# A planned order with other prices for transposes and landings, and earlier dates for loads

## The chip, the cores and the metric

The kernel runs on one core of a Trainium2 chip. The metric is the device time of one launch in microseconds (us), the median of three runs. Beside it there is the span of one profiled execution, from its first to its last instruction; it is about 2 us shorter than the time of that execution.

A core has five engines with instruction streams of their own: PE (TensorE, matmuls), ACT (ScalarE), DVE (VectorE), POOL (GpSimd) and SP (SyncE, which here only issues DMAs). Each executes its stream in order, so an instruction that waits holds up all that stand behind it on its engine.

## The reference, cut to what matters

```python
# q, k, v: 8 batches, 8 heads, 576 rows, 64 wide (float32)
phi = lambda x: np.where(x > 0, x, np.exp(x) - 1.0) + 1.0
q_p, k_p = phi(q), phi(k)
kv = einsum('bhsd,bhse->bhde', k_p, v)
z = sum(k_p, axis=2)
x = einsum('bhsd,bhde->bhse', q_p, kv) / (einsum('bhsd,bhd->bhs', q_p, z) + 1e-6)
# x as 4608 rows of 512; four experts, w1 512 x 1024, w2 1024 x 512
p = domain_probs / (domain_probs.sum(-1) + 1e-9)
out = sum over e of p[:, e] * (relu(x @ w1[e]) @ w2[e])
```

It is a linear attention whose output goes into a mixture of four experts, all of which are computed for every row and added with the weights p.

## The kernel before, in words

**Tiling.** Of the 576 rows of a batch, 512 form four chunks of 128; the other 64 (the "rest") of two batches share a tile. Attention runs per batch b and pair of heads pr: four pairs per batch. A pair loads k, v and q (`load_pair`, tiles kq and vs), takes Exp on ACT (L412), the rest of phi on DVE (L404, L405), casts v on ACT (L408), multiplies k and v on PE (L457, L460), copies the product on ACT (L470, L471), turns q so that its features lie on the partitions (qT, by a DMA transpose of SP at L443 for batches 2 to 7), multiplies again on PE (L481) and divides on DVE (L495 to L504) into x. `load_rest` and `rest_maps` do the same for the 64 rows (tiles kqr, vr; transpose at L334).

**Units.** From about 82 us on the experts run in 64 units (j, s, e): a block of 512 rows j, half of it s, expert e. `prep` scales two chunks by p on ACT (xp, L706) and turns them with one DMA transpose of SP (xT, L708). `xsums` makes sums of xT on DVE (xs, L724). `l1_seven` is the first matrix product with seven block products instead of eight (L746, eight matmuls each), with copies on ACT (L763), Relu on ACT (L760) and Relu with an addition on DVE (L766). `ssums` makes sums of its results on DVE (L808), and `l2_unit` is the second product, seven blocks of four matmuls (L822). After the fourth expert the sums are put together on DVE (L893 to L900) and stored by SP. Batches 0 and 1 and the first block of rows go another way, before 82 us.

**What sets the order.** Nothing is scheduled by hand. Each helper hands small pieces of work to the planner `Plan` by `pl.add(engine, duration, priority, function, r=..., w=..., move=..., after=...)`. `r` and `w` are keys of the buffers that are read and written, and give the dependencies. `Plan.order` then steps through time with a clock of its own: of the pieces that are ready, it takes the one that can start first, and of those within 0.1 us of it the one with the lowest priority. A piece with `move` is a DMA: after its issue (its duration) it goes through one common mover, and its users may start when it has landed. `after` is a time before which a piece isn't placed. The pieces are then emitted by their planned start, each engine in that order; POOL keeps the order of its adds. The planned times don't exist on the chip, only the order.

`T0` = 84 and `TU` = 6.4 are the planner's start of the first unit and its period; `U(n)` = T0 + n TU. `batch(b)` places the loads of batch b at `t - 8` and its attention from `t` on, where t counts backwards from the unit that first needs the batch.

**Buffers.** From batch 2 on, pairs alternate between two staging buffers (kq, vs). xp has two buffers, xT three, qT two.

Of the kernel before, what the change touches and what calls it, by code (L numbers as in the profile page):

```python
# [20 lines left out]
class Plan:  # L21
# [11 lines left out]
        self.wr = {}  # L33
        self.rd = {}

    def add(self, eng, dur, pri, fn, r=(), w=(), move=0.0, after=0.0):
        n = len(self.ops)
        deps = set()
        for key in r:
            if key in self.wr:  # L40
                deps.add(self.wr[key])
            self.rd.setdefault(key, []).append(n)
        for key in w:
            if key in self.wr:
                deps.add(self.wr[key])
            deps.update(x for x in self.rd.get(key, ()) if x != n)
        for key in w:
            self.wr[key] = n
            self.rd[key] = []
        self.ops.append(  # L50
            dict(eng=eng, dur=dur, pri=pri, fn=fn, deps=deps, move=move, after=after, w=w)
        )
        return n

    def order(self):
        ops = self.ops
        left = [len(o["deps"]) for o in ops]
        users = [[] for _ in ops]
        for n, o in enumerate(ops):
            for d in o["deps"]:  # L60
                users[d].append(n)
        free = {o["eng"]: 0.0 for o in ops}
        ready = {e: {} for e in free}
        fixed = {"POOL": [n for n, o in enumerate(ops) if o["eng"] == "POOL"]}
        at = [o["after"] for o in ops]
        mover = 0.0

        def release(n):
            ready[ops[n]["eng"]][n] = at[n]

        for n in range(len(ops)):
            if left[n] == 0:
                release(n)
        start = [0.0] * len(ops)
        for _ in ops:
            best = None
            for e, cand in ready.items():
                if e in fixed:
                    cand = {n: cand[n] for n in fixed[e][:1] if n in cand}
                if not cand:  # L80
                    continue
                t = max(free[e], min(cand.values()))
                if best is None or t < best[0]:
                    best = (t, e, cand)
            t, e, cand = best
            n = min(
                (n for n, x in cand.items() if x <= t + self.NEAR),
                key=lambda n: (ops[n]["pri"], n),
            )
            o = ops[n]  # L90
            del ready[e][n]
            if e in fixed:
                fixed[e].pop(0)
            start[n] = max(t, at[n])
            free[e] = done = start[n] + o["dur"]
            if o["move"]:
                mover = max(done + 1.2, mover) + o["move"]
                done = mover + 0.8
            o["start"], o["done"] = start[n], done
            for u in users[n]:  # L100
                lat = self.HOP if ops[u]["eng"] != e or o["move"] else 0.03
                at[u] = max(at[u], done + lat)
                left[u] -= 1
                if left[u] == 0:
                    release(u)
        return [ops[n] for n in sorted(range(len(ops)), key=lambda n: (start[n], n))]
# [3 lines left out]
def kernel(  # L110
# [10 lines left out]
    nc = tc.nc  # L121
# [10 lines left out]
    DC = Dm // P  # L132
# [5 lines left out]
    T0, TU = 84.0, 6.4  # L138

    pl = Plan()  # L140
# [36 lines left out]
    qTr = [sb(f"qTr{i}", [P, DC, P], FP16) for i in range(2)]  # L177
# [135 lines left out]
    def rest_maps(b, pe_mode, pri, parts=(0, 1)):  # L313

        par = b % 2
        rs = slice(par * R, par * R + R)
        ei = rot("ek", 2)
        er = ek_b[ei].rearrange("p i h c d -> p i (h c) d")

        def maps(i):  # L320
            o = kqpr[rs, i]
            nc.vector.tensor_scalar(o, kqr[rs, i], 0.0, 1.0, AO.max, AO.add)
            nc.vector.tensor_tensor(out=o, in0=er[rs, i], in1=o, op=AO.min)

        for i in parts:
            sk, ek, key = ("str", par, 2 * i), ("ek", ei, i), ("kpr", "qpr")[i]
            pl.add("ACT", 0.55, pri + i * 0.5, lambda i=i: nc.scalar.activation(
                er[rs, i], kqr[rs, i], AF.Exp), r=(sk,), w=(ek,))
            if i == 0:
                pl.add("ACT", 0.55, pri + 0.1, lambda: nc.scalar.copy(  # L330
                    vprs[par][rs, :, 0:D], vr[rs]), r=(("str", par, 1),), w=(("vpr", par),))
            pl.add("DVE", 0.92, pri + 0.5 + i * 0.5, lambda i=i: maps(i), r=(sk, ek), w=(key,))
        if not pe_mode:
            pl.add("SP", 0.45, pri + 1, lambda: nc.sync.dma_start_transpose(  # L334
                out=qTr[par][:, :, rs], in_=kqpr[rs, 1].rearrange("p h d -> p (h d)")),
                r=("qpr",), w=[("qTr", par, i) for i in range(DC)], move=1.2)

    def rest_late(pri):

# [42 lines left out]
    def attention(b, pr, pe_mode, pri, step, two=False):  # L382
# [35 lines left out]
        if pe_mode:  # L418

            tq, tk = (l2b[1].bitcast(FP16), "l2b1") if two else (tbank, "l2b3")  # L420

            def turn():
                for c in range(C):
                    nc.tensor.transpose(
                        out=tq[:, c * P : (c + 1) * P], in_=qp[:, c], identity=identh
                    )
                if two:
                    return
                nc.tensor.transpose(
                    out=tq[:, NT : NT + R],  # L430
                    in_=kqpr[rs, 1, hs].rearrange("p h d -> p (h d)"),
                    identity=identh[rs, rs],
                )

            pl.add("PE", 0.32, pri + 3 * step, turn,
                   r=(("kqp", pi, 1), "ident") + (() if two else ("qpr",)), w=(tk,))
            pl.add("ACT", 0.5, pri + 3.5 * step, lambda: nc.scalar.copy(
                qT.rearrange("p c t -> p (c t)"), tq[:, 0:NT]), r=(tk,), w=(("qT", ti),))
            if not two:
                pl.add("DVE", 0.2, pri + 3.5 * step, lambda: nc.vector.tensor_copy(  # L440
                    qTr[par][:, pr, rs], tq[:, NT : NT + R]), r=(tk,), w=(("qTr", par, pr),))
        else:
            pl.add("SP", 0.45, pri + 3 * step, lambda: nc.sync.dma_start_transpose(  # L443
                out=qT, in_=qp.rearrange("p c h d -> p (c h d)")),
                r=(("kqp", pi, 1),), w=(("qT", ti),), move=1.2)

        kvs_, ndk = slot[0], (("at",), ("at",))
        nds = [slot[0:3], slot[0:2]]
# [243 lines left out]
    def prep(n):  # L692

        j, s, e = units[n]
        xi, ti = n % 2, n % 3
        xp, xT = xp_b[xi], xT_b[ti]
        pri = U(n) - 7.0
        for c in range(2):
            cc = 2 * s + c
            if j < NJ - 1:  # L700
                src, ps = x_b[j % 2][:, cc, :], p_nat[:, j, cc, e : e + 1]
                r = [("x", j % 2, pr, cc) for pr in range(DC)] + ["pnat"]
            else:
                src, ps = xr_sb[:, cc, :], p_rest[:, cc, e : e + 1]
                r = [("xr", b, pr) for pr in range(DC) for b in (2 * cc, 2 * cc + 1)] + ["prest"]
            pl.add("ACT", 0.55, pri, lambda c=c, src=src, ps=ps: nc.scalar.activation(  # L706
                xp[:, c, :], src, AF.Copy, scale=ps), r=r, w=(("xp", xi, c),))
        pl.add("SP", 0.45, pri + 1, lambda: nc.sync.dma_start_transpose(  # L708
            out=xT.rearrange("p c k t -> p (c k) t"), in_=xp.rearrange("p c d -> p (c d)")),
            r=(("xp", xi, 0), ("xp", xi, 1)), w=(("xT", ti),), move=1.7)  # L710

    def xsums(n):
        xi, ti = n % 2, n % 3
        xT, xs = xT_b[ti], xs_b[xi]
        tt = nc.vector.tensor_tensor
        X = lambda i: ("xs", xi, i)
        for i, (o, a, b_, dur, d, r, w) in enumerate((
            (xs[:, 0:2], xT[:, 1].rearrange("p (a k) t -> p a k t", a=2), xT[:, :, 0:2],
             0.42, 0.9, (), (X(0), X(1))),
            (xs[:, 2], xT[:, 1, 2:4], xs[:, 0], 0.25, 1.8, (X(0),), (X(2),)),  # L720
            (xs[:, 3], xT[:, 0, 2:4], xs[:, 2], 0.25, 5.4, (X(2),), (X(3),)),
        )):
            pl.add("DVE", dur, U(n) + d - 1.0,
                   lambda o=o, a=a, b_=b_: tt(out=o, in0=a, in1=b_, op=AO.subtract),  # L724
                   r=(("xT", ti),) + r, w=w)
# [246 lines left out]
    def batch(b):  # L972

        due = U(8 * (b - 1)) - 8
        for pr in range(DC):
            t = due - (DC - pr) * 2 * TU
            if b == 2:
                t = T0 + 4 + 10.5 * pr
            load_pair(b, pr, "SP", t - 8, after=t - 8)
            if pr == 0:  # L980
                load_rest(b, "SP", t - 7, after=t - 7)
                rest_maps(b, False, t - 2)
# [56 lines left out]
```

## Time and profile before

| | |
|---|---|
| time, median of three runs | 508.55 us (507.77 to 510.18) |
| time of the profiled execution | 507.87 us |
| its span | 506.0 us |
| instructions | 14856 |
| TensorE clock granted | 0.997 |
| HBM read, written | 45.16 MB, 9.44 MB |
| SP's DMA queue (q1) | 51.53 MB, 46.0% of 16 engines' span |

The busy time of each engine is the sum over its instructions in the profiled execution. The busy tenths show 40 equal slices of the span, 12.65 us each; a 9 means 90% or more:

```profile
PE   2799999999999999999999999999999999999995
DVE  5787996989898989897979989888987676767664
ACT  5737667877888689758977887789776766676641
POOL 8856400000000000000000000000000000000000
```

Four stages can be seen: the weights come in on POOL's queue up to slice 5; from slice 6 or 7 to about slice 29 attention of batches 2 to 7 runs among the units; then units alone, with DVE and ACT less busy; and a short end.

### The profile page before, as it was taken

To read this page: it belongs to the slowest core of one execution; us is meant where nothing else is said; L and a number is where in the kernel's file an instruction comes from. 1 tells how busy PE (TensorE), PEld (TensorE's weight loads), DVE (VectorE), ACT (ScalarE), POOL (GpSimd) and SP (SyncE) were. 2 spreads that over 40 slices of the span, in tenths; PEclk is the share of its full clock that TensorE was granted. 3 is DMA by queue.
4 is the path that set the end of the run, shared out by engine and by line. 5 is a ranking of instruction groups with operands and counts; after the bars stand their busy time and mean duration, and the time that the engine had idled before them with its cause. 6 is when DMAs were issued, how large, how long until landed. Compare 5 with 4: busy or idle time off the path is not lost.

```text
span 506.0 us, 14856 instructions
## 1 busy us (share of the span) xinstructions
PE 483.4 (96%) x6008; PEld 424.3 (84%) x6008; DVE 409.1 (81%) x1036; ACT 368.3 (73%) x694; POOL 43.0 (8%) x68
## 2 busy tenths in 40 slices
PE   2799999999999999999999999999999999999995
PEld 1444546999989999998989999999999999999995
DVE  5787996989898989897979989888987676767664
ACT  5737667877888689758977887789776766676641
POOL 8856400000000000000000000000000000000000
PEclk9999999999999999999999999999999999999998
DMA  8999929667696767564666475566643232323221
GB/s 242 227 232 225 266 49 233 140 177 162 120 168 126 169 119 166 131 162 110 136 116 146 117 159 159 84 177 144 157 95 85 45 90 48 85 53 85 43 45 43
DMA packets 124006, 67.51 MB, mean 133 GB/s; under 512 B 94480, under 2 KB 117776, under 8 KB 123936
## 3 DMA queue, kind: packets, MB, share of 16 engines
q1 hardware_dynamic: 115056, 51.53, 46.0%
q0 software_dynamic: 8720, 14.76, 13.6%
q8 instruction: 47, 0.77, 0.6%
q10 hardware_dynamic: 160, 0.26, 0.1%
q14 instruction: 23, 0.19, 0.1%
HBM read 45.16 MB, written 9.44 MB: 108 GB/s over the span
## 4 chain that ended last, share of the span: by engine, by line
PE 72%; ACT 9%; DMA 7%; DVE 7%; issue 4%; SPq 2%; DVEq 0%; POOL 0%; POOLq 0%; ACTq 0%
PE l1b L746 29%; PE l2b L822 28%; PE l1b L594 6%; PE l2b L604 5%; DMA kq<-in_q_dram 2%; ACT xp L706 1%; ACT h L760 1%; SPq L232 1%; DMA kqr<-in_q_dram 1%; PE at L481 1%; DVE s L808 1%; DMA xT<-xp 1%; ACT ek L412 1%; DMA kqr<-in_k_dram 1%; PE at L457 1%
## 5 line engine op out<-in xcount | busy, mean ns | idle before, releaser
L746 PEld LDWEIGHTS <-w 128*128 128x128 f16 x2048 | 132.9, 98 | 6.7 <-issue 1.3
L822 PE MATMUL l2b<-w,h 128*128 128x256 f16 x768 | 114.4, 273 | 0.7 <-ACT h L760 0.6
L760 ACT ACTIVATE h<-l1b 128x512 f16<-128x512 f32 x128 | 76.7, 599 | 49.1 <-PE l1b L746 47.8
L822 PE MATMUL l2b<-t,s 128*128 128x256 f16 x768 | 112.3, 273 | 0.0
L746 PEld LDWEIGHTS <-w1x 128*128 128x128 f16 x1536 | 100.1, 98 | 7.5 <-issue 3.9
L822 PEld LDWEIGHTS <-s 128*128 128x128 f16 x1024 | 91.4, 98 | 6.9
L766 DVE CUSTOM_DVE_ANT_0 h<-l1b,p 128x512 f16<-128x512 f32 x64 | 44.2, 690 | 50.4 <-PE l1b L746 49.5
L746 PE MATMUL l1b<-xs,w1x 128*128 128x128 f16 x1024 | 77.7, 219 | 1.8 <-ACT l1b L763 1.7
L746 PE MATMUL l1b<-xs,w 128*128 128x128 f16 x1024 | 78.1, 219 | 1.0 <-ACT u L763 0.6
L706 ACT ACTIVATE xp<-x,p_nat 128x512 f16<-128x512 f16 x112 | 76.2, 721 | 3.3 <-DMA xT<-xp 3.0
L746 PE MATMUL l1b<-xT,w 128*128 128x128 f16 x1024 | 78.1, 219 | 0.1
L822 PEld LDWEIGHTS <-h 128*128 128x128 f16 x768 | 67.3, 98 | 5.9 <-ACT h L760 1.3
L808 DVE TENSOR_TENSOR s<-h 128x512 f16<-128x512 f16 x128 | 53.8, 420 | 1.4
L763 ACT COPY u<-l1b 128x512 f32<-128x512 f32 x64 | 37.5, 586 | 15.2 <-PE l1b L746 14.9
L766 DVE CUSTOM_DVE_ANT_0 h<-l1b,u 128x512 f16<-128x512 f32 x64 | 43.8, 684 | 1.4 <-PE l1b L746 1.1
L763 ACT COPY l1b<-l1b 128x512 f32<-128x512 f32 x64 | 36.8, 575 | 10.7 <-PE l1b L746 9.8
L412 ACT ACTIVATE ek<-kq 128x512 f16<-128x512 f32 x60 | 37.9, 631 | 7.8 <-DMA kq<-in_k_dram 4.4
L763 ACT COPY p<-l1b 128x512 f32<-128x512 f32 x64 | 37.5, 586 | 8.0 <-PE l1b L746 6.1
L724 DVE TENSOR_TENSOR xs<-xT,xs 128x256 f16<-128x256 f16 x128 | 36.9, 288 | 3.9
L746 PE MATMUL l1b<-xT,w1x 128*128 128x128 f16 x512 | 39.0, 219 | 0.3 <-ACT p L763 0.3
L822 PE MATMUL l2b<-w,s 128*128 128x256 f16 x256 | 38.4, 273 | 0.0
L405 DVE TENSOR_TENSOR kqp<-ek,kqp 128x512 f16<-128x512 f16 x64 | 27.2, 425 | 7.7 <-ACT ek L412 3.6
(114 smaller groups left out, 561.7 us busy)
## 6 DMA issues: line engine op xcount, KB each, us to landing
w<-in_moe_w_dram POOLq DMA_DIRECT2D x32, 256.0 KB, 7.6
out_dram<-ot SPq DMA_DIRECT2D x16, 512.0 KB, 4.6
kq<-in_k_dram SPq DMA_DIRECT2D x25, 256.0 KB, 3.0
vs<-in_v_dram SPq DMA_DIRECT2D x25, 256.0 KB, 3.2
kq<-in_q_dram SPq DMA_DIRECT2D x25, 256.0 KB, 4.0
kq<-in_k_dram POOLq DMA_DIRECT2D x5, 256.0 KB, 7.2
vs<-in_v_dram POOLq DMA_DIRECT2D x5, 256.0 KB, 6.6
kq<-in_q_dram POOLq DMA_DIRECT2D x5, 256.0 KB, 6.1
```

Of the source, the lines that this page charges most:

```text
L405: nc.vector.tensor_tensor(out=o, in0=ek[:, i], in1=o, op=AO.min)
L412: pl.add("ACT", 0.55, pri + i * step, lambda i=i: nc.scalar.activation(ek[:, i], kq[:, i], AF.Exp), r=(sk[i],), w=(("ek", ei, i),))
L594: nc.tensor.matmul(out=bank, lhsT=w1_sb[e][:, dc, fj * P : (fj + 1) * P], rhs=xt0[:, dc, :], start=(dc == 0), stop=(dc == DC - 1),)
L604: nc.tensor.matmul(out=bank, lhsT=hts[ht[fj]][:, c * P : (c + 1) * P], rhs=w2_sb[e][:, fj, :], start=(fj == 0), stop=(fj == FC - 1),)
L706: pl.add("ACT", 0.55, pri, lambda c=c, src=src, ps=ps: nc.scalar.activation(xp[:, c, :], src, AF.Copy, scale=ps), r=r, w=(("xp", xi, c),))
L724: lambda o=o, a=a, b_=b_: tt(out=o, in0=a, in1=b_, op=AO.subtract),
L746: nc.tensor.matmul(out=bank[:, fc * P : (fc + 1) * P], lhsT=wt[:, kc, fc * P : (fc + 1) * P], rhs=r[:, kc, :], start=(start and fc == 0 an ...
L760: return lambda: nc.scalar.activation(o, bank, AF.Relu)
L763: return lambda: nc.scalar.copy(o, bank)
L766: return lambda: nc.vector._custom_dve(TENSOR_ADD_SAT, out=o, in0=bank, in1=t, s0=BIG, s1=0.0)
L808: pl.add("DVE", 0.36, U(n + 1) + d - 0.5, lambda i=i, a=a, b_=b_, alu=alu: tt(out=s4[:, i], in0=a, in1=b_, op=alu), r=r, w=(Q(i),))
L822: nc.tensor.matmul(out=l2b[bank][:, half * HD : (half + 1) * HD], lhsT=a[:, c, :], rhs=w[:, c], start=(opens and first and c == 0), stop=( ...
```

## The change

Three things are changed, all of them numbers that the planner uses; the pieces of work and the buffers stay.

- A DMA transpose takes SP 1.25 us in the plan instead of 0.45. Its way to landing is counted as a lead of 0.2 (it was 1.2 for every DMA) and a move of 0.9 or 1.5 instead of 1.2 or 1.7. For every DMA, 0.6 is added at the end while the mover's clock is below 80, and 2.5 after that; it was 0.8.
- xp on ACT counts 0.6 instead of 0.55, and the three sums of `xsums` 0.45, 0.3 and 0.3 instead of 0.42, 0.25 and 0.25.
- The loads of batches 2 to 7 may be placed from `t - 14` on instead of `t - 8`, and have that as their priority. For batch 2, `t` is T0 + 1 + 9.5 pr instead of T0 + 4 + 10.5 pr.

```diff
-    def add(self, eng, dur, pri, fn, r=(), w=(), move=0.0, after=0.0):
+    def add(self, eng, dur, pri, fn, r=(), w=(), move=0.0, after=0.0, lead=1.2):
...
             if o["move"]:
-                mover = max(done + 1.2, mover) + o["move"]
-                done = mover + 0.8
+                mover = max(done + o["lead"], mover) + o["move"]
+                done = mover + (0.6 if mover < 80 else 2.5)
...
-            pl.add("SP", 0.45, pri + 3 * step, lambda: nc.sync.dma_start_transpose(
+            pl.add("SP", 1.25, pri + 3 * step, lambda: nc.sync.dma_start_transpose(
                 out=qT, in_=qp.rearrange("p c h d -> p (c h d)")),
-                r=(("kqp", pi, 1),), w=(("qT", ti),), move=1.2)
+                r=(("kqp", pi, 1),), w=(("qT", ti),), move=0.9, lead=0.2)
...
-            pl.add("ACT", 0.55, pri, lambda c=c, src=src, ps=ps: nc.scalar.activation(
+            pl.add("ACT", 0.6, pri, lambda c=c, src=src, ps=ps: nc.scalar.activation(
                 xp[:, c, :], src, AF.Copy, scale=ps), r=r, w=(("xp", xi, c),))
-        pl.add("SP", 0.45, pri + 1, lambda: nc.sync.dma_start_transpose(
+        pl.add("SP", 1.25, pri + 1, lambda: nc.sync.dma_start_transpose(
             out=xT.rearrange("p c k t -> p (c k) t"), in_=xp.rearrange("p c d -> p (c d)")),
-            r=(("xp", xi, 0), ("xp", xi, 1)), w=(("xT", ti),), move=1.7)
+            r=(("xp", xi, 0), ("xp", xi, 1)), w=(("xT", ti),), move=1.5, lead=0.2)
...
-             0.42, 0.9, (), (X(0), X(1))),
-            (xs[:, 2], xT[:, 1, 2:4], xs[:, 0], 0.25, 1.8, (X(0),), (X(2),)),
-            (xs[:, 3], xT[:, 0, 2:4], xs[:, 2], 0.25, 5.4, (X(2),), (X(3),)),
+             0.45, 0.9, (), (X(0), X(1))),
+            (xs[:, 2], xT[:, 1, 2:4], xs[:, 0], 0.3, 1.8, (X(0),), (X(2),)),
+            (xs[:, 3], xT[:, 0, 2:4], xs[:, 2], 0.3, 5.4, (X(2),), (X(3),)),
...
             if b == 2:
-                t = T0 + 4 + 10.5 * pr
-            load_pair(b, pr, "SP", t - 8, after=t - 8)
+                t = T0 + 1 + 9.5 * pr
+            load_pair(b, pr, "SP", t - 14, after=t - 14)
```

The transpose at L334 (rest, qTr) is changed in the same way as that at L443.

More of the change, by code (lines that the diff above doesn't have):

```diff
@@ L50, in add @@
         self.ops.append(
-            dict(eng=eng, dur=dur, pri=pri, fn=fn, deps=deps, move=move, after=after, w=w)
+            dict(eng=eng, dur=dur, pri=pri, fn=fn, deps=deps, move=move, after=after, lead=lead, w=w)
         )
@@ L333, in rest_maps @@
         if not pe_mode:
-            pl.add("SP", 0.45, pri + 1, lambda: nc.sync.dma_start_transpose(
+            pl.add("SP", 1.25, pri + 1, lambda: nc.sync.dma_start_transpose(
                 out=qTr[par][:, :, rs], in_=kqpr[rs, 1].rearrange("p h d -> p (h d)")),
-                r=("qpr",), w=[("qTr", par, i) for i in range(DC)], move=1.2)
+                r=("qpr",), w=[("qTr", par, i) for i in range(DC)], move=0.9, lead=0.2)
     def rest_late(pri):
@@ L705, in prep @@
                 r = [("xr", b, pr) for pr in range(DC) for b in (2 * cc, 2 * cc + 1)] + ["prest"]
-            pl.add("ACT", 0.55, pri, lambda c=c, src=src, ps=ps: nc.scalar.activation(
+            pl.add("ACT", 0.6, pri, lambda c=c, src=src, ps=ps: nc.scalar.activation(
                 xp[:, c, :], src, AF.Copy, scale=ps), r=r, w=(("xp", xi, c),))
-        pl.add("SP", 0.45, pri + 1, lambda: nc.sync.dma_start_transpose(
+        pl.add("SP", 1.25, pri + 1, lambda: nc.sync.dma_start_transpose(
             out=xT.rearrange("p c k t -> p (c k) t"), in_=xp.rearrange("p c d -> p (c d)")),
-            r=(("xp", xi, 0), ("xp", xi, 1)), w=(("xT", ti),), move=1.7)
+            r=(("xp", xi, 0), ("xp", xi, 1)), w=(("xT", ti),), move=1.5, lead=0.2)
     def xsums(n):
```

## The prediction

> **What bounds the kernel now.** I read first the engine shares, then busy time by stretch, then who waits for whom, then the chain that ended last, then the transfers.
>
> Engine shares, first lines of the page:
>
> ```profile
> PE 483.4 (96%) x6008; PEld 424.3 (84%) x6008; DVE 409.1 (81%) x1036; ACT 368.3 (73%) x694; POOL 43.0 (8%) x68
> ```
>
> PE (matmuls) bounds the span of 506.0 us. Only its idle time can be won, so the question is where that lies. Busy time by stretch (columns PE, PEld, DVE, ACT, POOL, clock, DMA share, GB/s):
>
> ```profile
> 82.20:366.00 283.80, 279.42 (x3799) 261.93 (x3798) 250.27 (x652) 230.97 (x441) 0.00 (x0) 1.00 0.66 146
> 366.00:493.60 127.60, 127.60 (x1743) 121.14 (x1742) 89.81 (x219) 84.37 (x150) 0.00 (x0) 1.00 0.31 67
> ```
>
> From 366 us, when no batch is loaded any more, PE has no idle time at all. While loads, attention and the MoE units run together (82.2 to 366) it is idle 283.80 - 279.42 = 4.38 us. Waits in that stretch, for ACT, DVE and PE:
>
> ```profile
> ACT ek L412 <- DMA kq<-in_q_dram: 3.1, 6, 0.9
> ACT ek L412 <- DMA kq<-in_k_dram: 2.6, 4, 1.0
> ACT vp L408 <- DMA vs<-in_v_dram: 2.1, 2, 1.2
> ACT xp L706 <- DMA xT<-xp: 1.1, 1, 1.1
> ...
> PE l1b L746 <- ACT l1b L763: 1.5, 5, 0.4
> ...
> PEld L746 <- issue: 4.9, 13, 0.8
> ```
>
> ACT stands still for landings, 3.1 + 2.6 + 2.1 + 1.1 = 8.9 us, and PE waits mostly for ACT's copies, not for DMA itself. One such place, in the chain that ended last (start, length, what):
>
> ```profile
> 248.48 0.48 SPq L232
> ...
> 249.00 5.17 DMA kq<-in_q_dram
> ...
> 254.30 0.55 issue
> 254.85 0.61 ACT h L760
> ```
>
> A q load was issued at 249.00 and landed 5.17 us later. The Exp that needs it is ahead of a Relu of the MoE in ACT's order, so the Relu, and PE after it, came late. In the stretch 250.4 to 263.2 PE has 0.32 us of idle time for it.
>
> **Visible and hidden loss.** A matmul is shown 219 ns long, while eight L746 matmuls follow each other in 0.445 us (0.89 for 16 in the chain), so up to 219 - 56 = 163 ns of each gap is covered by a modelled end. The whole loss: in the stretch without attention the same chain row recurs at 406.10, 430.83, 455.56 and 480.30, 24.73 us for four units, 6.183 each. 64 units are 395.7 us. An attention pair adds 0.30 + 0.17 + 0.11 = 0.58 us (five, three and two matmuls, by the distance to the next start in the timeline), 24 pairs 13.9. The first L746 starts at 82.23; the last four matmuls start at 499.97 and take 0.44, so 418.2 us in all. The loss is 418.2 - 395.7 - 13.9 = 8.6 us, 1.96 times the visible 4.38. This is the most that a better order after 82 us can bring.
>
> **What the Trainium skill says.** "DMA: Bandwidth & Descriptors", section "Rules for kernel authors": issue a DMA early, do compute, wait for it late. Here the trace shows it broken at 249.00. The same page, "Anatomy of one DMA", says that DMA engines wait for no semaphore; the issuing sequencer does. The trace agrees: SP's queue was held 99.7 us in 35 waits of L708 for L746, and whatever stood behind was held too. "Perfetto Trace Analysis", "Summary: the profiler window per engine type", calls the end of a TensorE instruction estimated; 219 ns shown against 56 ns of pace agrees.
>
> **The change, part by part.** No instruction is added or removed; only the planner's numbers change, and with them the order. By the built order, of the planner's entries 340 of 1091 on PE, 334 of 663 on ACT, 421 of 847 on DVE and 136 of 209 on SP take another place; POOL's 62 stay.
>
> *SP's price of a transpose, 0.45 to 1.25.* The trace:
>
> ```profile
> L708 SPq DMA_TRANSPOSE xT<-xp x64: 1231/1240/2084, 74.3 to 477.7; - x64
> L443 SPq DMA_TRANSPOSE qT<-kqp x24: 1189/1209/2182, 89.9 to 377.1; - x24
> ```
>
> So 1.25 is right and 0.45 was not: 94 transposes (64, 24, 6) by 0.79 are 74 us of SP time that the old plan didn't know, and it put loads behind transposes as if they cost little. The chip pays nothing new: the time was always taken.
>
> *Landings.* For an xT transpose the planner counted 0.45 + 1.2 + 1.7 + 0.8 = 4.15 us from issue to landing and now 1.25 + 0.2 + 1.5 + 2.5 = 5.45; for one load 0.5 + 1.2 + 0.7 + 0.8 = 3.2, now 4.9. Measured to landing (median): 3.2 for xT, 3.1 for qT, 3.0, 3.2 and 4.0 for the loads on SP, at most 6.7 (xT) and 6.5 (kq after 84 us). The new values lie between median and worst, so users stand later behind their transfers. Cost on the chip: nothing by itself.
>
> *Loads 6 us sooner in the plan (14 instead of 8 ahead of their use; batch 2 starts 3 us earlier too).* I count it in the built order, in PE steps: one step is eight L746 or four L822 matmuls, 0.44 us. For each load of batches 2 to 7 I take the last PE step that SP or ACT must have seen before the load, and before the first ACT instruction that uses it; the difference is its lead. The kq/q/v load at 249.00 had a lead of 10 steps (4.4 us, under the 5.17 it took); now 38. Over the loads after the first three pairs of batch 2, 24 of 78 had 14 steps (6.2 us) or fewer; now 9, the least 11. The median goes from 17 to 22.5. For the transposes qT to PE the median goes from 22 to 26.5, xT to DVE from 17 to 19. This takes away most of the ACT waits for landings.
>
> *Queues that they pass.* The same 72 pair loads and 18 remainder loads go out, SP issues at 0.47 to 0.65 us each. On SP most triples of loads now stand ahead of the xT or qT transpose that they stood behind. A triple holds the next transpose for 3 x 0.5 = 1.5 us, plus any wait for its staging buffer. Behind it wait xT (DVE L724, PE L746) and qT (PE L481). xT's shortest usual lead stays 12 steps = 5.3 us against a median landing of 3.2, so 2 us of delay is free. The first triple of batch 2 moves ahead of the first two xT transposes; these waited for xp until 74.28 anyway, so I cost it at nothing. The early stores of ot move behind loads; ot is next written some 25 us later: nothing.
>
> *ACT's and DVE's order.* xp at 0.6 instead of 0.55 (measured 0.721), xs at 0.45 and 0.3 (0.418, 0.288): closer, small. Three ACT entries of the first pair of batch 2 (631, 627, 631 ns) leave the crowd after 83 us, where ACT is busy 11.62 of 12.80, for the 3.3 us in which it stood idle between 77 and 83.
>
> *The sum.* The 4.38 us visible are, by stretch: 0.79 up to 97, 1.46 between 122 and 161, 2.13 after. For the first I leave 0.6 (ACT stays crowded there); for the second 0.8, since loads of batch 3, which go out there, still have only 11 to 12 steps; for the third 0.7, where nearly all leads grow to 18 and more. Left: 2.1, won: 2.28 visible, times 1.96 = 4.5 us. Span 506.0 - 4.5 = 501.5; the time of that execution was 507.87, inside the three runs (507.77 to 510.18). From the median 508.55 - 4.5 = **504.1 us**. Bounds: at best 0.5 is left, (4.38 - 0.5) x 1.96 = 7.6 us, 501.0.
>
> **The rivals.** *A. ACT's crowding, not the landings, makes PE late.* For it: PE waits for "L763" and "issue", with landings right ahead only in 1.1 us (0.2, 0.5 and 0.4 after qT and xT). Against: ACT is 81% busy in that stretch, and it never holds PE up after 366. Then only 1.1 x 1.96 = 2.2 us are won, or nothing: 506.4 to 508.5, no difference. I put it at 507.0.
>
> *B. Slower: loads ahead of transposes hold SP until their staging buffer is free, and xT comes late.* For it: SP executes in order and its waits are long (L708 up to 4.8 us for PE). Against: only 0.4 us of PE's waits stand behind xT now. It decides once a triple delays an xT by more than the 2.1 us of slack (5.3 - 3.2). 21 xT transposes have a lead of 14 steps or fewer in the new order; if each then cost PE 0.2 us, 4.2 us are lost and nothing won: 512.8.
>
> *C. The order changes, but no load goes out sooner, because the staging buffer is freed late (two buffers).* The buffer is free after the q-part of the pair two before; in the built order the PE step that SP must have seen falls by 8 to 32 for 20 of 24 triples, so I give it little, inside A.
>
> **How the numbers follow.** Forecast (faster by 2.5 to 8.6 us) 0.70, A with C 0.19, B 0.11. A measurement of this kernel tells about 0.5% (2.5 us) from no change; so faster 0.70, same 0.19, slower 0.11. Range: 501.0 from the bound above; at the top 508.0, which takes in most of A and leaves out its end and B.
>
> **What would show it.** Right: PE idle between 82 and 366 falls from 4.38 to about 2; ACT's waits for kq and vs from 7.8 to under 3 us; the load of the example is issued well ahead. First stretch to 97 still with idle time. Wrong: PE or DVE wait for xT or qT (B); ACT's waits for landings are gone but PE's idle time is not (A).

## The result, and the profile after

The changed kernel takes 502.58 us (median of four runs, 502.13 to 504.01) against 509.37 of the kernel before on the same chip: a ratio of 0.9871, with a 95% interval of 0.983 to 0.9912. The span of the profiled execution fell from 506.0 to 500.4 us. The forecast was 504.1.

The engine shares of the changed kernel, from the page:

```profile
PE 480.9 (96%) x6008; PEld 423.5 (85%) x6008; DVE 409.4 (82%) x1036; ACT 368.1 (74%) x694; POOL 42.4 (8%) x68
```

Each engine executes as many instructions as before. Busy time by stretch of the changed kernel (columns PE, PEld, DVE, ACT, POOL, clock, DMA share, GB/s):

```profile
82.20:366.00 283.80, 283.14 (x3882) 267.22 (x3881) 254.24 (x662) 234.67 (x450) 0.00 (x0) 1.00 0.66 148
366.00:490.00 124.00, 124.00 (x1689) 117.54 (x1688) 84.95 (x206) 81.20 (x142) 0.00 (x0) 1.00 0.30 62
```

PE's idle time between 82.2 and 366 us is 283.80 - 283.14 = 0.66 us; it was 4.38. The waits of ACT for landings and of PE, changed kernel (us in total, times, longest), are taken from 84 to 366 us, as those in the prediction are:

```profile
ACT xp L706 <- DMA xT<-xp: 0.4, 1, 0.4
ACT ek L412 <- DMA kq<-in_q_dram: 0.3, 1, 0.3
...
PE l1b L746 <- ACT l1b L763: 0.3, 1, 0.3
...
PEld L746 <- issue: 1.1, 5, 0.3
```

Of the 8.9 us that ACT stood still for kq, vs and xT, 0.7 are left. The chain that ended last, by engine, of the changed kernel and then of the kernel before:

```profile
PE 90%; DMA 3%; ACT 3%; DVE 2%; issue 1%; POOL 1%; DVEq 0%; POOLq 0%; ACTq 0%
```

```profile
PE 72%; ACT 9%; DMA 7%; DVE 7%; issue 4%; SPq 2%; DVEq 0%; POOL 0%; POOLq 0%; ACTq 0%
```

The chain now runs through PE almost without leaving it. The load of the example in the prediction (its q was issued at 249.00, its Exp waited for it until 254.19) goes out here at 235.96. SP and then ACT, by time, changed kernel:

```profile
234.82 0.57 SPq L232 DMA_DIRECT2D kq<-in_k_dram  x1
...
235.96 0.47 SPq L232 DMA_DIRECT2D kq<-in_q_dram  x1
```

```profile
249.82 0.63 ACT L412 ACTIVATE ek<-kq 128x512 f16<-128x512 f32 x1
```

Its Exp starts 13.9 us after the issue, 8.7 us more than before, and finds the data there.

Where the gain lies on PE: its stretch from the first L746 to the end of the last matmul was 82.23 to 500.41 and is 82.55 to 494.74 (the last four start at 494.30 and take 0.44), 412.2 instead of 418.2 us. Less the 409.6 us of work worked out in the prediction, the loss is 2.6 us, and was 8.6. Won: 6.0 us, of which the start that came 0.3 us later takes a little back. The pace without attention is the same in both kernels (24.73 us for four units, here from 449.89 to 474.62), and PE is not idle between 366 and 490 us in either, so the gain lies before 366 us.

### The profile page after: what moved, and what is told of

It reads as the page before. It is cut to its first block, busy times and chain, and to the rows that moved or that the text cites. A ratio compares the mean times of both kernels' runs of the same rounds, so it can differ in the third digit from the quotient of the medians.

```text
span 500.4 us, 14836 instructions
## 1 busy us (share of the span) xinstructions
PE 480.9 (96%) x6008; PEld 423.5 (85%) x6008; DVE 409.4 (82%) x1036; ACT 368.1 (74%) x694; POOL 42.4 (8%) x68
## 3 DMA queue, kind: packets, MB, share of 16 engines
q0 software_dynamic: 8720, 14.76, 13.9%
## 4 chain that ended last, share of the span: by engine, by line
PE 90%; DMA 3%; ACT 3%; DVE 2%; issue 1%; POOL 1%; DVEq 0%; POOLq 0%; ACTq 0%
PE l1b L746 39%; PE l2b L822 37%; PE l2b L604 5%; PE l1b L594 5%; DMA w<-in_moe_w_dram 2%; PE at L481 2%; PE at L457 1%; DMA vr<-in_v_dram 1%; ACT xp L706 1%; DVE ot L661 1%; ACT h L760 0%; DVE ot L888 0%; ACT ek L412 0%; PE at L460 0%; ACT p L763 0%
## 5 line engine op out<-in xcount | busy, mean ns | idle before, releaser
L746 PEld LDWEIGHTS <-w 128*128 128x128 f16 x2048 | 132.4, 98 | 4.8
L746 PEld LDWEIGHTS <-w1x 128*128 128x128 f16 x1536 | 99.9, 98 | 5.1 <-issue 1.5
L746 PE MATMUL l1b<-xs,w1x 128*128 128x128 f16 x1024 | 78.1, 219 | 0.5 <-ACT l1b L763 0.3
L746 PE MATMUL l1b<-xT,w 128*128 128x128 f16 x1024 | 78.1, 219 | 0.0
L746 PE MATMUL l1b<-xs,w 128*128 128x128 f16 x1024 | 78.1, 219 | 0.0
L706 ACT ACTIVATE xp<-x,p_nat 128x512 f16<-128x512 f16 x112 | 76.4, 720 | 1.2 <-DMA xT<-xp 0.4
L724 DVE TENSOR_TENSOR xs<-xT,xs 128x256 f16<-128x256 f16 x128 | 36.9, 288 | 4.1 <-DVE xs L724 0.5
L412 ACT ACTIVATE ek<-kq 128x512 f16<-128x512 f32 x60 | 37.8, 631 | 2.4 <-DMA kq<-in_k_dram 1.9
L746 PE MATMUL l1b<-xT,w1x 128*128 128x128 f16 x512 | 39.0, 219 | 0.1
```

The lines of the kernel that those rows point to most:

```text
L412: pl.add("ACT", 0.55, pri + i * step, lambda i=i: nc.scalar.activation(ek[:, i], kq[:, i], AF.Exp), r=(sk[i],), w=(("ek", ei, i),))
L706: pl.add("ACT", 0.6, pri, lambda c=c, src=src, ps=ps: nc.scalar.activation(xp[:, c, :], src, AF.Copy, scale=ps), r=r, w=(("xp", xi, c),))
L746: nc.tensor.matmul(out=bank[:, fc * P : (fc + 1) * P], lhsT=wt[:, kc, fc * P : (fc + 1) * P], rhs=r[:, kc, :], start=(start and fc == 0 an ...
```

## The experiments

Three theories. **L**: loads land after the instruction that needs them is due; ACT stands still, its copies and Relus behind come late, and PE waits. **C** (rival A of the prediction): the order crowds ACT and DVE, whatever the landings do. **N**: the order of the kernel before was just a bad draw of the planner, and any other would do better.

Beside time and waits I use one more reading, from the timelines of SP and ACT: the time from the issue of each of the 24 k loads of batches 2 to 7 to the start of its Exp, and how many of the 72 loads of k, q and v have less than 5 us. "PE idle" is given for 82.2 to 97 and for 97 to 366 us, and "ACT, DVE" are their waits for landings from 97 to 366 us. Median times of the kernel before in these comparisons were 509.37 to 510.24. Times and ratios are medians of several executions, the other columns come from one profiled execution each. Single executions of the kernel before lay between 506.11 and 512.97 us, and the profiled one took 507.87, so 1 or 2 us of PE idle time between two kernels prove little: m2 and n1 show more of it than the kernel before, at the same time or a shorter one.

| kernel | time, us | ratio (95%) | PE idle, us | ACT, DVE, us | k: median to Exp; of 72 under 5 us |
|---|---|---|---|---|---|
| before | 509.37 | 1 | 0.79 + 3.59 | 9.7 | 4.1; 48 |
| changed | 502.58 | 0.9871 (0.983-0.9912) | 0.48 + 0.18 | 0.7 | 7.2; 7 |
| e1, dates alone | 503.19 | 0.9855 (0.9806-0.9904) | 1.42 + 0.98 | 2.8 | 5.1; 24 |
| e2, prices alone | 504.02 | 0.9881 (0.9843-0.9919) | 0.57 + 2.14 | 0.3 | 6.0; 13 |
| m1, margin alone | 505.56 | 0.9898 (0.9865-0.9932) | 1.22 + 2.19 | 0.3 | 7.2; 3 |
| m2, SP price alone | 509.85 | 0.9998 (0.9968-1.0027) | 1.02 + 5.56 | 11.3 | 4.2; 47 |
| d6, dates at 6 | 505.70 | 0.9899 (0.9857-0.9942) | 0.40 + 2.30 | 5.0 | 4.9; 32 |
| n1, another hop | 509.20 | 0.9976 (0.9957-0.9995) | 0.22 + 4.75 | 8.1 | 4.3; 43 |
| e5, no margin | 503.62 | 0.9887 (0.9852-0.9922) | 1.84 + 0.24 | 1.9 | 4.7; 30 |
| e7, dates at 20 | 503.75 | 0.9896 (0.9856-0.9936) | 1.93 + 0.46 | 0 | 7.4; 2 |

### The two halves of the change

e1, from the kernel before:

```diff
-                t = T0 + 4 + 10.5 * pr
-            load_pair(b, pr, "SP", t - 8, after=t - 8)
+                t = T0 + 1 + 9.5 * pr
+            load_pair(b, pr, "SP", t - 14, after=t - 14)
```

> Only the dates of the loads are changed (14 instead of 8 ahead, batch 2 earlier); prices of transposes, landings, xp and xs as before. In the built order the loads keep short leads (25 of 78 at 14 PE steps or fewer, before 24, after 9), but places where ACT or DVE has more work than the PE steps ahead of its user give it time fall as in the changed kernel (before 28, here 9, after 10). Theory L (late landings cost PE its time): little is won, 507 to 509 us, ACT waits for kq and vs 5 us or more, PE idle between 82 and 366 us 3 us or more. Theory C (crowded ACT and DVE cost it): nearly all is won, 502 to 504 us, PE idle under 1.5 us.

e2, from the changed kernel:

```diff
-                t = T0 + 1 + 9.5 * pr
-            load_pair(b, pr, "SP", t - 14, after=t - 14)
+                t = T0 + 4 + 10.5 * pr
+            load_pair(b, pr, "SP", t - 8, after=t - 8)
```

> Only the prices are changed (transposes 1.25 on SP, landings with 2.5, xp, xs); the dates of the loads stay at 8 ahead. Built order: leads long (4 of 78 at 14 steps or fewer), crowded places 21 of before's 28. Theory L: nearly all is won, 502 to 504.5 us, ACT waits for kq and vs under 2 us. Theory C: little is won, 506.5 to 509 us, though ACT waits for landings fall.

Each half alone brings nearly the whole gain; their intervals overlap with that of the whole. For e1 theory C had the time (502 to 504), though PE was idle for 2.40 us and not under 1.5; for e2 theory L had it (502 to 504.5). So neither stands as written. But the measured waits say why e1 works: ACT waits 2.8 us for landings instead of 9.4 (0.6 of it for kqr, whose loads stay at `t - 7` in the change, too), and the k loads have a median of 5.1 us to their Exp instead of 4.1. My count of leads in PE steps (25 short ones, as before) had said that nothing would change there. It counts what an instruction must have seen, not when it is issued, and was wrong as a measure.

What prices alone leave after 97 us is 2.14 us, and PE stands behind no landing there. PE in e2, by time, with the idle time before the instruction in brackets:

```profile
138.11 0.41 PE L457 MATMUL at<-vp,kqp 128*128 128x130 f16 x4 [1.46 <-DVE kqp L405]
```

DVE is late here: from 125.9 us to that kqp it works with hardly a gap, and in this stretch no engine has waited for a load. With two places of 0.34 us that follow within 5 us it makes up all of the 2.14 us. With dates alone the stretch from 122.4 to 161 has no idle time on PE. So a part of C stays, and it is the dates that remove it.

### One part alone, one against the sense, and one without meaning

m1, m2, d6 and n1 are the kernel before with one edit each, shown in this order (m2 also has the `lead` argument of `add` and the transpose at L334 as in the change):

```diff
-                done = mover + 0.8
+                done = mover + (0.6 if mover < 80 else 2.5)
```

> The kernel before with one edit: landings count 0.6 or 2.5 instead of 0.8 (the margin); transposes keep 0.45 on SP, loads their 8. Built order: 1 of 78 loads at 14 PE steps or fewer (before 24), crowded places of ACT and DVE 39 (before 28). Theory L (late landings): 502 to 504.5 us. Theory C (crowding): 508 us or more. Theory N (the order of before was just a bad draw, any other does better): 502 to 506 us.

```diff
-            pl.add("SP", 0.45, pri + 3 * step, lambda: nc.sync.dma_start_transpose(
+            pl.add("SP", 1.25, pri + 3 * step, lambda: nc.sync.dma_start_transpose(
...
-                r=(("kqp", pi, 1),), w=(("qT", ti),), move=1.2)
+                r=(("kqp", pi, 1),), w=(("qT", ti),), move=0.9, lead=0.2)
...
-            r=(("xp", xi, 0), ("xp", xi, 1)), w=(("xT", ti),), move=1.7)
+            r=(("xp", xi, 0), ("xp", xi, 1)), w=(("xT", ti),), move=1.5, lead=0.2)
```

> The kernel before with one edit: transposes at 1.25 on SP, lead 0.2, moves 0.9 and 1.5; no margin, loads at 8, xp and xs as before. Built order: short leads as before (25 of 78), qT's median lead to PE falls from 22 to 19 steps, crowded places 23. Theory L: 507 to 510 us, ACT waits for kq and vs stay at 6 us or more. Theory C: 506 to 508.5. Theory N: 502 to 506 us.

```diff
-            load_pair(b, pr, "SP", t - 8, after=t - 8)
+            load_pair(b, pr, "SP", t - 6, after=t - 6)
```

> The kernel before with one edit against the sense of the change: loads at 6 ahead instead of 8. Built order: 13 of 78 short leads, the median 20 steps, crowded places 19: the planner moves the users with the loads. Theory L by the plain word (loads later are worse): 510 us or more; by the counted leads 504 to 507. Theory C: 504 to 507. Theory N: 502 to 506.

```diff
-    HOP = 0.28
+    HOP = 0.27
```

> The kernel before with one edit that has nothing to do with the change: the planner's hop between engines 0.27 instead of 0.28. Built order: 23 of 78 short leads (before 24), crowded places 22 (before 28). Theories L and C: within 2 us of the kernel before. Theory N: 502 to 506 us.

m1: 505.56 us. C fails (it had the most crowded places by my count, 39, and 508 or more was expected); L has the sense, and its number was 1 us too good: landings are gone (0.3 us), but 2.19 us of PE idle time remain between 122.4 and 161, as in e2. m2: nothing, 0.9998. The truer price of a transpose on SP wins nothing when the landings stay at 0.8, and ACT and DVE wait for landings no less than before, 11.3 us against 9.7 (for kq and vs alone 4.8 us, less than the 6 or more that L expected). d6 was faster, not slower. The planner moved the users, too: the k loads have 4.9 us to their Exp, more than with the earlier date of 8. A date in the plan isn't a date on the chip. The time of d6 fits L by the counted leads, C and N alike, so it doesn't decide between them. n1: 509.20; an order that is different without a reason (23 short leads, before 24) is 0.24% faster and no more. With m2 it speaks against N: two other orders do nearly as the kernel before does, so not any other order does better.

Among the ten kernels of the table, the time from issue to Exp sets the slow orders (4.1 to 4.3 us, 509 us or more) apart from the others (4.7 us or more, under 506), but it doesn't rank those: m1 has 7.2 us and takes 505.56, e5 has 4.7 and takes 503.62. The prices of xp and xs were not tried alone, and neither was the earlier start of batch 2.

### The landing alone, in an unchanged order

s1 is the kernel before and s2 the changed kernel, each with this edit. Both orders stay as they are; from batch 3 on most of k, q and v isn't loaded.

```diff
+            src = t[b, hs, 0:NT].rearrange("h (p c) d -> p h c d", c=C)
+            if b >= 3:
+                o, src = o[0:16], src[0:16]
```

> The kernel before, every engine in the same order; but from batch 3 on the pair loads of k, q and v bring 16 of the 128 partitions only (32 KB instead of 256), the others keep older data. So only the landing gets shorter. Theory L: with landings near 2 us ACT's waits for kq and vs after 135 us vanish and most of the loss with them, 503 to 506 us. Theory C: the order is as crowded as before, 507 to 509.5 us.

> The control: the changed kernel with the same small loads from batch 3 on. Theory L: there is no wait for landings left to take away, 502 to 503.5 us, within 0.3% of the changed kernel; so what less traffic brings by itself is small. If small loads help in another way, it is faster than 501.5 us too.

The transfers of kq in s1 after 135 us, and then the stretch after the first 15 us of units in s1 and in the kernel before:

```profile
DMA to landing us min/median/max: 1.8/2.2/4.0
```

```profile
97.00:366.00 269.00, 267.89 (x3675) 253.89 (x3673) 239.63 (x628) 221.69 (x424) 0.00 (x0) 1.00 0.45 95
```

```profile
97.00:366.00 269.00, 265.41 (x3606) 249.12 (x3604) 236.47 (x618) 218.02 (x416) 0.00 (x0) 1.00 0.65 143
```

With full loads kq's landing took 2.7, 3.7 and 6.5 us (least, median, most) in the same time. Shorter by 1.5 us in the median, it takes ACT's waits from 9.4 to 0.5 us and PE's idle time after 97 us from 3.59 to 1.11; the time is 503.26 us, 0.9885 (0.9853 to 0.9916). The order, with all its crowding, is that of the kernel before. The control s2 takes 502.49 us, 0.9869 (0.9837 to 0.9901), as the changed kernel does with full loads: where nothing waits for a landing, smaller loads win nothing. In s1 the transposes land a little sooner too (the median of qT falls from 3.1 to 2.4 us, the longest xT from 6.7 to 4.8), so s1 prices landings as a whole, not those of the loads alone. This settles it for L in the main: shorter landings alone bring 1.15% of the time where the whole change brings 1.29%. Of s1's 1.11 us that remain, 1.00 lie between 122.4 and 161, where e2 and m1 had theirs; ACT waits for no landing there.

### SP's order apart from the others

e3 keeps PE, ACT, DVE and POOL of the kernel before and gives SP the order of the changed kernel; e4 keeps them of the changed kernel and gives SP that of the kernel before, as nearly as the dependencies allow. `merged` takes SP's pieces from a list and those of the others from the plan.

```diff
         todo = pl.order()
+        todo = merged(pl.ops, todo, SP_ORDER)
```

> PE, ACT, DVE and POOL in the order of the kernel before; SP alone in the order of the changed kernel. Leads long (9 of 78 at 14 steps or fewer), crowded places unchanged at 28; xT's lead to DVE falls from a median of 17 to 14.5 steps. Theory L: most is won, 503 to 505.5 us. Theory C: as before, 507 to 509.5 us, while ACT waits for kq and vs fall under 3 us.

> PE, ACT, DVE and POOL in the order of the changed kernel; SP follows the order of the kernel before as far as this doesn't lock the engines. Leads short (57 of 78 at 14 steps or fewer, some none), crowded places 10. Theory L: slower than before, 512 us or more, ACT waits for kq and vs over 15 us. Theory C: the short leads cost something too, but less than the crowding did: 503 to 508 us.

e3 takes 565.28 us, 1.1074 (1.102 to 1.1128), and e4 605.28 us, 1.1843 (1.1772 to 1.1914). No theory had such a number for e3. e4 lies within L's open range (512 or more, ACT's waits for kq and vs over 15 us; they are 49.7 us), but PE also waits 14.8 us for qT. Waits in e3 (its L735, L737, L753 are L706, L708, L724 of the kernel before), then in e4 (L447 is L412), between 84 and 366 us:

```profile
ACT xp L735 <- DMA xT<-xp: 39.5, 11, 7.1
...
DVE xs L753 <- DMA xT<-xp: 19.0, 5, 6.2
```

```profile
ACT ek L447 <- DMA kq<-in_k_dram: 40.1, 14, 6.8
```

One place of e3. The third xT transpose goes out at 93.29, and ACT waits 7.06 us for it; in the kernel before it went out at 83.04. SP and ACT of e3, then SP of the kernel before:

```profile
93.29 1.26 SPq L737 DMA_TRANSPOSE xT<-xp  x1
```

```profile
97.90 1.33 ACT L735 ACTIVATE xp<-x,p_nat 128x512 f16<-128x512 f16 x2 [7.06 <-DMA xT<-xp]
```

```profile
83.04 1.88 SPq L708 DMA_TRANSPOSE xT<-xp  x1
```

In SP's new order a qT transpose and three loads stand before this xT. The qT transpose waits for DVE's kqp, and in the old order of DVE that comes at 90 us. So an SP queue is held by what a transpose was moved behind, as rival B feared, but not by what B named. B named loads that wait for a staging buffer; what holds SP longest in e3 is qT transposes that wait for DVE. Their waits (L472) sum to 113.1 us between 84 and 366 us (56.4 in the kernel before), those of loads (L261) to 9.1. The two longest of SP in e3:

```profile
SPq L472 <- DVE s L837: 53.1, 8, 10.5
SPq L472 <- DVE kqp L434: 21.7, 3, 10.5
```

In the changed kernel the same SP order does no harm, since DVE makes that kqp sooner: qT goes out at 80.88 and xT at 83.88. e4 shows the other side, loads behind transposes that their users can't wait for. The granted clock was lower in both, 0.968 and 0.95 in the profiled executions, and how much of the loss is the clock's was not told apart from the waits.

### Without the margin, and earlier still

e5 and e7, from the changed kernel:

```diff
-                done = mover + (0.6 if mover < 80 else 2.5)
+                done = mover + 0.8
```

> The changed kernel without the margin: landings count 0.8 as before, the rest as changed. Dates alone gave 0.9855 of the time of before, the margin alone 0.9898. Theory L: as dates alone with a few waits for landings of 2 to 4 us in sum, 502.5 to 505 us. If the price of transposes on SP hurts without the margin (alone it won nothing): 505 to 508 us.

```diff
-            load_pair(b, pr, "SP", t - 14, after=t - 14)
+            load_pair(b, pr, "SP", t - 20, after=t - 20)
```

> The changed kernel with loads at 20 ahead instead of 14. Theory L: no waits for landings are left to win, 502 to 503.5 us; PE idle between 97 and 366 us stays under 0.5. Theory B (loads ahead of transposes hold SP until a staging buffer is free): xT comes late in places, 504 us or more, and DVE or PE wait for xT by 1 us or more.

e5 takes 503.62 and e7 503.75 us; their intervals hold the ratio of the changed kernel. Both fit L, though e7 lies 0.25 us above its range. In e5 waits for landings of 1.9 us come back on ACT after 97 us, but PE's idle time after 97 us is 0.24. In e7 no engine waits for a landing between 82.2 and 366 us, xT's among them: B doesn't come in at 20 either. Both lose more in the first stretch, 1.84 and 1.93 us against 0.48, in e7 mostly at one place:

```profile
PE l1b L746 <- DVE xs L724: 1.4, 1, 1.4
```

None of these kernels is shown to beat the changed one.

## Why the prediction was right

**What bounds the kernel, and where the loss lies.** Right. The gain is PE's idle time, visible and hidden, between 82 and 366 us.

**The cause.** Late landings on ACT, as the prediction had it against rival A, which s1 and s2 show in an unchanged order. A keeps a part, by DVE's crowding as well as ACT's: between 122 and 161 us PE is idle for 2.15 us behind no late landing in e2, and for 1.00 of the 1.46 us of the kernel before when the landings are short (s1). The prediction had put that stretch down to loads with short leads. All 1.46 us went, so about 1 us of the 3.7 us of visible idle time that were won came by another way than it said. Its 1.1 us for rival A was misread, too: 0.2 us are PE's own, the other 0.9 are idle time of the weight loads (PEld).

**Part by part.** The price of transposes on SP: the chip pays nothing new, right; alone it doesn't win anything either (m2). The landings' margin: I wrote that it costs nothing by itself and places users later, which is what m1 does (k loads to Exp: 4.1 to 7.2 us). The dates: they help, but not as counted. The lead in PE steps had the sense for the whole change and for d6, and missed e1. The two halves don't add up, 1.2 and 1.45% against 1.3% together: they remove largely the same waits.

**The sum.** 4.5 us was forecast; the span fell by 5.6, and the ratio makes 509.37 x 0.0129 = 6.6 us of the time. Two terms were mis-sized. One is what would be left of the visible idle time: 0.6, 0.8 and 0.7 us by stretch, 2.1 in all. Measured: 0.48 up to 97 us, nothing between 122 and 161 and 0.18 in the rest, 0.66 in all. So 3.72 us of visible idle time were won and not 2.28. The other is the factor for the hidden part: 1.96 was too large, since 6.0 us were won in all and 6.0 / 3.72 = 1.61. It isn't a constant either: the changed kernel loses 2.6 us by the same count while 0.66 are visible. The two errors pull in opposite directions, and that 4.5 came so near is in part luck. The 0.3 us by which the first unit starts later are not in the sum; I didn't follow up their cause.

**The slower rival.** That xT comes late behind a held SP queue is real in e3, and the price of 0.2 us for each transpose was far too low for an order that doesn't fit (11 waits of ACT of 3.6 us in the mean). But it is mostly qT transposes that hold the queue there, not loads. It doesn't come in with this change, in which the planner gives all engines their order at once: neither DVE nor PE waits for xT or qT.

**What was to show it.** PE idle "about 2" was 0.66; ACT's waits for kq and vs "under 3" were 0.3; the load of the example went out 13 us sooner; the first stretch kept most of the idle time that is left, 0.48 of 0.66.

## What to carry to other kernels

Where engines execute in order and one queue feeds the one that feeds PE, read the time from each load's issue to its first use against the landing times of the same loads: here a median of 4.1 us against landings of 2.7 to 6.5 cost most of 1.3%, and orders with 5 to 7 us won most or all of it. A planner gets there by a margin on its landings or by earlier dates; here either brought most of the gain. Moving the DMAs alone, in the order of another plan, cost 10.7 and 18.4%. To tell a late transfer from a bad order, shorten the transfer, leave the order alone, and make the same edit in the changed kernel as a control.

## What else the runs show of the hardware

Loads of 32 KB instead of 256 KB landed in 2.0 and 2.2 us instead of 3.4 and 3.7 (medians of vs and kq, s1 against the kernel before, 135 to 366 us): with an eighth of the bytes the median fell by about 1.5 us, and about 2 us remained. In e3 PE also ran at a lower granted clock where it waited: between 97.0 and 122.4 us it was busy for 16.82 of 25.40 us, and the clock was 0.80; in the kernel before it was busy all the time there, and the clock was 1.00. That isn't the same in every stretch: between 82.2 and 97.0 us PE of e3 was busy for 10.12 of 14.80 us at a clock of 1.00. What sets it is open.
